# The last store of a fused attention and MLP kernel, issued as two row halves by two queues

## The chip, the cores and the metric

The kernel runs on one core of one Trainium2 chip. The metric is the device time of one execution in microseconds (us), as the median of several runs; lower is better. The profile gives a second number, the span from the first to the last instruction, which is about 1.4 us less than the time (203.0 against 204.4 for the profiled run of the kernel before).

"Tail" below is my word for the stretch from the end of the last VectorE addition to the end of the span. On the path that ends last it holds nothing but the last store and the wait for it, and it can be read from each profile without the scatter of the 200 us ahead of it.

## The reference

```python
x  = A_x                                   # (1, 2048, 640), bfloat16
xn = layernorm(x)
out = x + linear_attention(xn, wqkv, wo)   # 32 heads
        + gelu(xn @ w1 + b1) @ w2 + b2     # hidden width 1536
```

Only the end of this matters here: the output is 2048 token rows of 640 columns, and the last tile of 128 rows is added up and stored in three pieces.

## The kernel before

One planner records instructions for five engines and adds a semaphore wait wherever one engine needs another's result. The stores of the last tile are made in `out_last`: three column pieces of 320, 192 and 128 columns. Each has its matmuls into one bank, one addition by VectorE into `out_l`, and one store that SyncE issues.

```python
def out_last(t):
    xb(t)
    lo = 0
    for i, w in enumerate((HW, 3 * 64, P)):          # 320, 192, 128 columns
        b = take(1)
        hs = slice(lo, lo + w)
        o = out_l[:, hs]
        ...                                          # 17 matmuls into bank b      (L726)
        Pl.ins(v, lambda e, ...: e.tensor_tensor(    # the addition                (L729)
            out=o, in0=bank(b, 0, w), in1=x_res[:, t, hs], op=ALU.add), ...)
        stores.append(Pl.ins("sync", lambda e, hs=hs, o=o:   # the store           (L732)
            e.dma_start(ov[t * P:(t + 1) * P, hs], o), reads=[r_outl[i]], dma=True))
...
for ev in stores[:-1]:
    Pl.wait_event("gpsimd", ev)      # GpSimd waits for all stores but the last
Pl.wait_event("sync", stores[-1])    # SyncE waits for the last                    (L108)
```

The three tiles ahead of the last go through `out_fin`, which makes one addition of 640 columns and one store of 128 rows each, some 5 us apart.

## Time and profile before

| kernel before | |
|---|---|
| time, median of 3 runs | 204.94 us (204.71 to 204.94) |
| span of the profiled run | 203.0 us |
| TensorE busy | 98% of the span |
| last addition ends | 201.54 us |
| tail | 1.51 us |
| last store, from the start of its issue to landing | 1.44 us |

The prediction below shows the lines and how they are read. In a line of the timeline the first number is the start, the second the duration; "SPq" and "ACTq" are the sequencers of SyncE and ScalarE, which issue DMAs. A DMA is "landed" when the last of its steps on its semaphore has come.

### The profile page before, as it was taken

Reading aid. Unit: us, or ns where it says so; the run is one execution under the profiler, and the core shown is the slowest. Engines: PE = TensorE matmul, PEld = TensorE weight load, DVE = VectorE, ACT = ScalarE, POOL = GpSimd, SP = SyncE. Lnnn points to the kernel's source line nnn. Section 1 sums busy time; section 2 is a strip of 40 time slices with the busy share of each in tenths; the row PEclk is TensorE's granted clock in tenths of the full one; section 3 lists DMA queues with packets and bytes.
Section 4 is the critical chain, followed back from the end, with each engine's and each line's share of the span. In section 5 each row is a group of like instructions: output and inputs, shape, how many; then the busy total and the mean of one; then the engine's idle time right before and its main releaser. Section 6 shows DMA issues by size and latency. Waiting matters only on the chain.

```text
span 203.0 us, 3442 instructions
## 1 busy us (share of the span) xinstructions
PE 199.1 (98%) x1317; PEld 121.8 (60%) x1329; DVE 123.0 (61%) x238; ACT 72.8 (36%) x139; POOL 14.4 (7%) x43
## 2 busy tenths in 40 slices
PE   7999999999999999999999999999999999999996
PEld 2799884444457777777756565444444444447775
DVE  4789682000006888999468899896793385356322
ACT  3589886666666544211143596100000000000000
POOL 3145443000000000000000000000000000000000
DMA  5975985999800000000289435115551966084402
GB/s 174 360 259 114 149 181 110 351 275 294 188 0 3 0 0 3 0 0 3 43 273 322 77 66 108 39 29 125 110 116 39 207 106 129 27 196 93 161 32 65
DMA packets 48134, 24.51 MB, mean 121 GB/s; under 512 B 33702, under 2 KB 48118, under 8 KB 48118
## 3 DMA queue, kind: packets, MB, share of 16 engines
q1 hardware_dynamic: 46094, 23.44, 46.4%
q10 hardware_dynamic: 2024, 0.86, 1.7%
q8 instruction: 10, 0.16, 0.3%
q14 instruction: 6, 0.05, 0.1%
HBM read 12.72 MB, written 2.62 MB: 76 GB/s over the span
## 4 chain that ended last, share of the span: by engine, by line
PE 96%; DVE 1%; DMA 1%; issue 0%; DVEq 0%
PE ps L748 27%; PE ps L375 25%; PE ps L524 11%; PE ps L557 11%; PE ps L569 11%; PE ps L690 7%; PE ps L726 2%; PE ps L407 1%; DMA xPK<-in_A_x_dram 1%; DVE stats L331 1%; PE ps L583 1%; PE ps L601 1%; PE ps L396 0%; DVE xn_tm L389 0%; DVE out_l L729 0%
## 5 line engine op out<-in xcount | busy, mean ns | idle before, releaser
L375 PE MATMUL ps<-xnT,W 128*128 128x256 bf16 (+2 forms) x372 | 50.2, 296 | 0.2
L375 PEld LDWEIGHTS ps<-xnT,W 128*128 128x128 bf16 x375 | 32.4, 98 | 17.3
L379 ACT ACTIVATE HG<-ps,b1c 128x256 bf16<-128x256 f32 (+2 forms) x75 | 37.3, 522 | 13.1 <-PE ps L375 11.3
L748 PE MATMUL ps<-HG,W 128*128 128x512 bf16 x177 | 39.2, 379 | 0.2
L748 PEld LDWEIGHTS ps<-HG,W 128*128 128x128 bf16 x180 | 17.6, 98 | 21.2
L569 PE MATMUL ps<-xnT,Wqkv 128*128 128x512 bf16 x96 | 22.2, 379 | 0.2
L524 PE MATMUL ps<-Wqkv,xnT 128*128 128x320 bf16 x160 | 21.9, 299 | 0.0
L557 PE MATMUL ps<-xPK,xn_tm 128*128 128x320 bf16 x160 | 21.9, 299 | 0.0
L524 PEld LDWEIGHTS ps<-Wqkv,xnT 128*128 128x128 bf16 x160 | 15.7, 98 | 6.2
L557 PEld LDWEIGHTS ps<-xPK,xn_tm 128*128 128x128 bf16 x160 | 15.7, 98 | 6.1
L754 DVE SCALAR_TENSOR_TENSOR W<-ps,b2c,xnT 128x512 bf16<-128x512 f32 x15 | 11.3, 751 | 8.9 <-PE ps L748 8.8
L748 PE MATMUL ps<-PQ,Msb 128*128 128x512 bf16 x73 | 16.4, 379 | 0.1
L569 PEld LDWEIGHTS ps<-xnT,Wqkv 128*128 128x128 bf16 x100 | 11.3, 118 | 8.5
L331 DVE BATCH_NORM_STATS2 stats<-xPK 128x6 f32<-128x320 bf16 x32 | 13.7, 468 | 4.4 <-DMA xPK<-in_A_x_dram 4.4
L508 ACT ACTIVATE xn_tm<-ps 128x512 bf16<-128x512 f32 x20 | 11.9, 597 | 9.4 <-PE ps L569 8.7
L511 DVE SCALAR_TENSOR_TENSOR PQ<-ps,xn_tm 128x512 bf16<-128x512 f32 x20 | 13.8, 692 | 2.1
L508 ACT ACTIVATE ek<-ps 128x640 bf16<-128x640 f32 x16 | 11.2, 703 | 9.2 <-PE ps L524 9.2
L511 DVE SCALAR_TENSOR_TENSOR xPK<-ps,ek 128x640 bf16<-128x640 f32 x16 | 13.2, 825 | 1.7
L516 DVE CAST b2c<-out_l 128x5 f32<-128x5 bf16 x1 | 0.2, 172 | 22.4 <-DMA out_l<-b2bc 22.4
L748 PEld LDWEIGHTS ps<-PQ,Msb 128*128 128x128 bf16 x75 | 7.3, 98 | 8.8
L618 DVE SCALAR_TENSOR_TENSOR xn_tm<-PQ,z_sb,xn_tm 128x512 f32<-128x512 bf16 x16 | 12.0, 750 | 0.4
L544 DVE TENSOR_TENSOR Msb<-Msb,xPK 128x640 f32<-128x640 f32 x14 | 11.6, 826 | 0.5
(64 smaller groups left out, 136.1 us busy)
## 6 DMA issues: line engine op xcount, KB each, us to landing
xPK<-in_A_x_dram SPq DMA_DIRECT2D x5, 640.0 KB, 6.9
Wqkv<-in_A_wqkv_dram SPq DMA_DIRECT2D x3, 800.0 KB, 7.0
W<-in_B_w_dram SPq DMA_DIRECT2D x1, 1920.0 KB, 14.8
out_dram<-xPK SPq DMA_DIRECT2D x3, 640.0 KB, 3.6
W<-in_B_w_dram SPq DMA_DIRECT2D x2, 640.0 KB, 6.7
xPK<-in_A_x_dram SPq DMA_DIRECT2D x4, 320.0 KB, 5.9
Wo<-in_A_wo_dram SPq DMA_DIRECT2D x1, 750.0 KB, 11.6
xPK<-in_A_x_dram SPq DMA_DIRECT2D x4, 160.0 KB, 4.4
```

Of the source, the lines that this page charges most:

```text
L331: Pl.ins(v, lambda e: e.bn_stats(stats[:, s, 6 * h:6 * h + 6], x_in[:, t, h * HW:(h + 1) * HW]), reads=[r_x[t]], writes=[r_stats[s][h]])
L375: Pl.ins("tensor", [(lambda e, k=k: e.matmul(bank(b, 0, w), W1[:, k, jb * P:(jb + 1) * P], xnT[:, k, tok], start=(k == 0), stop=(k == DT - ...
L379: Pl.ins("scalar", lambda e: e.activation(HG[:, jb, tok], bank(b, 0, w), ACT.Gelu_apprx_tanh, bias=b1c[:, jb:jb + 1]), reads=[B_[b], r_b1c ...
L508: Pl.ins("scalar", lambda e: e.activation(e2, src, ACT.Exp), reads=br, writes=[re])
L511: Pl.ins(v, lambda e: e.scalar_tensor_tensor(out=d2, in0=src, scalar=0.0, in1=e2, op0=ALU.max, op1=ALU.add), reads=br + [re], writes=[res_ ...
L524: fns.append(lambda e, k=k, h=h, b=b, t=t: e.matmul(bank(b + h, 0, HW), xnT[:, k, t * P:(t + 1) * P], Wqkv[:, k, D + h * HW:D + (h + 1) * ...
L544: Pl.ins(v, lambda e, t=t: e.tensor_tensor(out=zsum, in0=zsum, in1=PK[:, t, :], op=ALU.add), reads=[r_PK[t], r_zsum], writes=[r_zsum])
L557: Pl.ins("tensor", [(lambda e, t=t, h=h, b=b, f=f: e.matmul(bank(b + h, 0, HW), xn_tm[:, t, f * P:(f + 1) * P], PK[:, t, h * HW:(h + 1) * ...
L569: Pl.ins("tensor", [(lambda e, k=k, j=j, b=b: e.matmul(bank(b), Wqkv[:, k, j:D:DT], xnT[:, k, cc], start=(k == 0), stop=(k == DT - 1))) fo ...
L618: Pl.ins(v, lambda e: e.scalar_tensor_tensor(out=yv[c % 2], in0=pq, scalar=z_sb[:, j:j + 1], in1=yv[c % 2], op0=ALU.mult, op1=ALU.add), re ...
L690: return lambda e: e.matmul(bank(b + h, 0, HW), l, r[:, h * HW:(h + 1) * HW], start=(i == 0), stop=(i == JT + DT - 1))
L748: Pl.ins("tensor", lambda e, l=l, r=r, i=i: e.matmul(bank(b), l, r, start=(i == 0), stop=(i == JT + DT - 1)), reads=rd, writes=[B_[b]], ma ...
```

## The change

Its intent is to shorten the tail. The last store, 128 rows of 128 columns, is cut into two halves of 64 rows. ScalarE issues one, SyncE the other, and each queue waits for its own, so that each moves half the bytes.

```diff
-                stores.append(Pl.ins("sync", lambda e, hs=hs, o=o: e.dma_start(ov[t * P:(t + 1) * P, hs], o),
-                                     reads=[r_outl[i]], dma=True))
+                if i < 2:
+                    stores.append(Pl.ins("sync", ...))          # as before
+                    continue
+                for h, eng in ((1, "scalar"), (0, "sync")):
+                    a = h * (P // 2)
+                    stores.append(Pl.ins(eng, lambda e, hs=hs, a=a: e.dma_start(
+                        ov[t * P + a:t * P + a + P // 2, hs], out_l[a:a + P // 2, hs]), reads=[r_outl[i]], dma=True))
...
-        for ev in stores[:-1]:
+        for ev in stores[:-2]:
             Pl.wait_event("gpsimd", ev)
+        Pl.wait_event("scalar", stores[-2])
         Pl.wait_event("sync", stores[-1])
```

More of the change, by code (lines that the diff above doesn't have):

```diff
@@ L731, in out_last @@
                     reads=[B_[b], r_xb[t]], writes=[r_outl[i]])
-                stores.append(Pl.ins("sync", lambda e, hs=hs, o=o: e.dma_start(ov[t * P:(t + 1) * P, hs], o),
-                                     reads=[r_outl[i]], dma=True))
+                if i < 2:
+                    stores.append(Pl.ins("sync", lambda e, hs=hs, o=o: e.dma_start(ov[t * P:(t + 1) * P, hs], o),
+                                         reads=[r_outl[i]], dma=True))
+                    continue
[3 more added lines that the diff above has]
+                        ov[t * P + a:t * P + a + P // 2, hs], out_l[a:a + P // 2, hs]), reads=[r_outl[i]], dma=True))
         def den_parts(c, lo, hi):
```

## The prediction

> **What bounds the kernel now.** I read the views from the coarse to the fine: the busy shares and the chain on the profile page, then the chain of waits in its last microseconds, then the timeline, the wait list of the store queue and the packets of the last store. The page first: columns of its first part are busy microseconds, share of the span, instruction count; the chain is a list of shares.
>
> ```profile
> PE 199.1 (98%) x1317; PEld 121.8 (60%) x1329; DVE 123.0 (61%) x238; ACT 72.8 (36%) x139; POOL 14.4 (7%) x43
> ...
> PE 96%; DVE 1%; DMA 1%; issue 0%; DVEq 0%
> ```
>
> The reader is to see that TensorE sets the time of nearly everything (98% busy, 96% of the chain), and that the change touches none of its instructions: the comparison of instruction orders has the same TensorE, VectorE and GpSimd rows on both sides, line numbers apart. The only additions are one store on ScalarE's queue (64 rows x 128 columns), and the last SyncE store shrinking from 128x128 to 64x128. So only the end can move. The chain of waits for the last 8 us (start, duration, what) and the timeline there (start, duration, engine, line, operation) end as follows.
>
> ```profile
> 196.55 4.67 PE ps L726 x51
> 201.22 0.02 issue
> 201.25 0.29 DVE out_l L729
> ```
>
> ```profile
> 201.25 0.29 DVE L729 TENSOR_TENSOR out_l<-ps,xPK 128x128 bf16<-128x128 f32 x1 [0.59 <-PE ps L726]
> ```
>
> The last addition ends at 201.54; the span is 203.0. Between lies the last store alone: 1.50 us, 0.7% of the span. That is the most that any change to this store could save, and 2% of the time would be 4.1 us. What fills it is in three further views: the wait list of the SyncE queue, the DMA summary of 201.1 to 202.0, and the DMA summary of 202.35 to 202.75 (40 slices of 10 ns each; the digits are tenths of busy DMA engines).
>
> ```profile
> SPq L108 <- DMA out_dram<-out_l: 1.1, 1, 1.1
> ```
>
> ```profile
> out_dram<-out_l SPq DMA_DIRECT2D x1, 32.0 KB, 1.4
> ```
>
> ```profile
> DMA  0000044376588959986694651221100000000000
> ...
> DMA packets 144, 0.03 MB, mean 82 GB/s; under 512 B 144, under 2 KB 144, under 8 KB 144
> ```
>
> SyncE starts the issue at 201.57, spends 0.33 us on it, then waits 1.1 us for the landing. The packets show when: none before 202.39, all done by 202.66, so 0.82 us pass from the start of the issue to the first packet, 0.27 us with packets, and 0.35 us from the last packet to the last of the 16 semaphore steps at 203.01 (1.44 us in all, "1.4" in the line). Only the 0.27 us depends on the size of the store. The 144 packets are 128 rows of 256 B and 16 small ones, one for each of 16 DMA engines; the packet records show a row each 14 ns on one engine, so 8 rows take 0.11 us on an engine, and the engines' last packets are staggered over 0.15 us. The larger stores say the same: 80, 48 and 32 KB land after 1.6, 1.5 and 1.4 us.
>
> **What the Trainium skill says.** The page "DMA: Bandwidth & Descriptors", section "Rules for kernel authors", speaks of exactly this: two transfers to disjoint partition halves "serialize", since both halves spray over all 16 DMA engines. The same page, "Issuing engines are not separate DMA queues", says that starting from several engines saves only the sequencer's issue time. Here one store is split, so there is not even a second issue to save: 0.33 us stays in front of each half. The page's section "Why a DMA increments its semaphore by 16 and not by 1" makes each engine used post its own step, so two halves post 32 rather than 16; the trace has 16 small packets in the 144, which agrees. Its section "Anatomy of one DMA" puts most of a fixed cost of about 2.0 us into the receipt of the written bytes (for another issue path); this trace shows 1.44 in all and only 0.35 after the last packet, so the measured pieces are used.
>
> **The change, part by part.** SyncE's half: the issue stays at 0.33 us (the stores of 1280, 640, 384 and 256 B rows all took 332 to 345 ns when nothing was queued ahead, so bytes don't set it; that rows don't either is my estimate). An engine then has 4 rows instead of 8, which saves 4 x 14 ns = 0.06 us, or up to half the packet stretch, 0.13 us, if the stagger halves too. So this half lands about 1.31 to 1.38 us after issue, earlier than now. This gain counts only if the other half is no later.
>
> ScalarE's half: the trace has pairs issued by both queues at the same moment, with equal size. In the timeline the starts are 176.94 and 176.95, and the DMA summary of 176.9 to 179.6 (queue, bytes, median from issue to landing) has
>
> ```profile
> xn_tm<-rden SPq DMA_DIRECT2D x2, 32.0 KB, 1.9
> xn_tm<-rden ACTq DMA_DIRECT2D x2, 32.0 KB, 2.2
> ```
>
> and the view of that line of the program (min/median/max ns in the issuing queue) has
>
> ```profile
> L643 SPq DMA_DIRECT2D xn_tm<-rden x10: 591/606/1284, 131.6 to 177.6; - x10
> L643 ACTq DMA_DIRECT2D xn_tm<-rden x6: 627/648/856, 141.7 to 177.6; - x6
> ```
>
> ScalarE's issue itself is 0.04 us longer, but its transfer lands 0.3 us later. Where the rest comes from is in two windows that stop early, at 1.50 us after the pair's issue and at 1.35 us after an issue by ScalarE that has no SyncE issue within 0.4 us of it (168.71; this one 64 KB):
>
> ```profile
> q1 hardware_dynamic: 127, 0.03, 9.0%
> q14 instruction: 1, 0.01, 2.1%
> ```
>
> ```profile
> q1 hardware_dynamic: 544, 0.13, 47.3%
> q10 hardware_dynamic: 3, 0.00, 0.4%
> ```
>
> Queue 1 is SyncE's, queue 10 ScalarE's. In the pair, SyncE's queue has moved 127 packets by then and ScalarE's none: its first packet comes 1.54 us after issue, against 1.27 us for SyncE's. Alone, ScalarE's first packets are there after 1.33 us. So ScalarE has a lateness of its own of about 0.06 us, and 0.21 us more when SyncE issues 128 rows in the same moment: something behind the two issues takes them one after the other. I take 0.21 us for 128 rows to be half, 0.10 us, for 64 rows (an estimate; if it is a fixed turn it stays 0.21).
>
> Sum for the half that lands last: 1.44 now, less 0.06 to 0.13 for the halved packets (middle 0.09), plus 0.06 for ScalarE, plus 0.10 for the turn: 1.51 us, so +0.07 us. Its packets also share the engines with SyncE's last ones and 16 more semaphore steps are posted: at the 12 ns that lie between the present steps (16 in 0.18 us), they would cost 0.19 us if both batches came at once; staggered by the turn, most of that is hidden, and I add 0.02. Total +0.09 us. The waits themselves cost nothing new: each queue waits for its own half at the place where SyncE waited anyway, GpSimd still waits for the other 8 stores (its wait for the last of them was over at 202.3), and ScalarE has had no work since 178.5. Nothing earlier moves. Predicted time: 204.94 + 0.09 = about 205.0 us.
>
> **The rivals.** First, the halves really run in parallel: each queue has its own generation and half the packets, so the store ends 0.06 to 0.13 us earlier, and ScalarE's own 0.06 us takes half of that: 204.85 to 204.95. For it speaks that the DMA engines are not full (mean 37.5% in the window above); against it the 0.3 us lateness of every simultaneous pair. Second, the turn is fixed or ScalarE pays what the pairs show in full: 1.44 - 0.09 + 0.30 = 1.65, +0.2 us, 205.15. For it: the pairs' 2.2 against 1.9; against it: those pairs move 128 rows a queue. Third, the end of the program becomes another: the closing exchange between engines may take longer when ScalarE comes last instead of idling there. The trace has no such case; I allow 0.1 us either way. In none of these does an engine become the bound, since TensorE ends at 201.2 in all.
>
> **Range and chances.** The mechanisms span 204.85 to 205.15. The three runs of before lie between 204.71 and 204.94, so a run differs by 0.2 us from the next for nothing, and another session can shift both; I widen to 204.65 to 205.35. Faster by over 2% would need 4.1 us out of a 1.5 us tail: 0.5%. Slower by over 2% would need a transfer of 32 KB to take four times as long: 0.5%. Within 2%: 99%.
>
> **What would show it.** Right, if in the profile of the changed kernel the last addition still ends 0.29 us after its start near 201.25; SyncE's 16 KB lands after 1.3 to 1.4 us, and ScalarE's after 1.45 to 1.6, with its first packets about 0.1 us or more behind SyncE's; and the span is 203.0 to 203.2. The parallel rival is right if both land at 1.4 or below. The fixed turn is right if ScalarE's first packet is 0.27 us behind. I am wrong in kind if ScalarE's issue starts late, if the last addition moves, or if the span and the time part company by more than before (204.4 for the profiled run with a span of 203.0).

## The result and the profile after

The changed kernel took 205.57 us (median of 6 runs, 205.17 to 206.25) against 204.92 us (6 runs, 204.71 to 205.18) for the kernel before. The ratio is 1.0034 with a 95% interval of 1.0014 to 1.0054. By the 2% mark that is "the same", but it is slower clear of the noise, by some 0.65 us, and it lies outside my range, which ended at 205.35.

TensorE is still busy for 98% of the span. The chain of waits of the changed kernel for the last microseconds:

```profile
197.40 4.68 PE ps L726 x51
...
202.10 0.29 DVE out_l L729
```

The 51 matmuls take 4.68 us where they took 4.67, and the addition still takes 0.29 us. So the work of the end is unchanged, but it starts 0.85 us later. Following the offset between the two traces back instruction by instruction, it arises in the first 16 us, in VectorE's wait for loads of x. Here is that group in the wait list of the first 17 us (total us, times, longest), first of the kernel before, then of the changed one:

```profile
DVE stats L331 <- DMA xPK<-in_A_x_dram: 2.4, 2, 1.9
```

```profile
DVE stats L331 <- DMA xPK<-in_A_x_dram: 3.5, 2, 2.0
```

No instruction was changed there. The repeat below shows that most of this part, at least, is chance and not what the change costs. The tail is what it costs. In this profile it is 2.12 us, from 202.39 to 204.51, against 1.51. The timeline and the DMA summary (KB, us from issue to landing) give:

```profile
202.41 0.56 SPq L738 DMA_DIRECT2D out_dram<-out_l  x1
202.42 0.58 ACTq L738 DMA_DIRECT2D out_dram<-out_l  x1
```

```profile
out_dram<-out_l SPq DMA_DIRECT2D x1, 16.0 KB, 1.8
out_dram<-out_l ACTq DMA_DIRECT2D x1, 16.0 KB, 2.1
```

Both issues start within 4 ns of each other, at once after the addition, so neither queue is late to wake. But a half of 16 KB lands later (1.8 us) than the whole of 32 KB did (1.4 us), and ScalarE's half another 0.3 us later. When the packets move is in the DMA summary of 203.59 to 203.99 (slices of 10 ns, digits as in the prediction): SyncE's from 203.63 to 203.86, and ScalarE's, of which the window holds the first 42, from 203.90 on.

```profile
DMA  0000326252756533631431201000000325344665
```

Put together with the packet and semaphore records of both traces, in us:

| piece | before, 128 rows, SyncE | changed, 64 rows, SyncE | changed, 64 rows, ScalarE |
|---|---|---|---|
| issue | 0.333 | 0.558 | 0.582 |
| end of issue to first packet | 0.492 | 0.656 | 0.897 |
| first to last packet | 0.262 | 0.219 | 0.217 |
| last packet to last semaphore step | 0.357 | 0.352 | 0.356 |
| sum, issue to landing | 1.444 | 1.785 | 2.052 |

Below I call the pause between issue and first packet "generation", and the stretch from the last packet to the last semaphore step "receipt". These are names for measured stretches; what happens inside them is not shown.

Halving the rows did shorten the packet stretch, by 0.04 us. The issue became longer by 0.23 us and the pause to the first packet by 0.16 us, for SyncE's half alone; ScalarE's comes a further 0.27 us behind. 0.34 + 0.27 = 0.61 us, which is the growth of the tail and, within noise, of the time (0.65 by the medians, 0.70 by the ratio).

### The profile page after: what moved, and what is told of

Its sections match the earlier page's. It is cut to its first block, busy times and chain, and to the rows that moved or that the text cites. A ratio compares the mean times of both kernels' runs of the same rounds, so it can differ in the third digit from the quotient of the medians.

```text
span 204.5 us, 3456 instructions
## 1 busy us (share of the span) xinstructions
PE 199.8 (98%) x1329; PEld 121.6 (59%) x1329; DVE 122.9 (60%) x238; ACT 73.0 (36%) x139; POOL 14.4 (7%) x43
## 4 chain that ended last, share of the span: by engine, by line
PE 90%; DMA 5%; DVE 2%; SPq 1%; issue 0%; POOL 0%; DVEq 0%
PE ps L754 27%; PE ps L375 21%; PE ps L524 11%; PE ps L557 11%; PE ps L569 11%; PE ps L690 7%; DMA xPK<-in_A_x_dram 3%; PE ps L726 2%; DMA xnT<-xn_tm 1%; DVE stats L331 1%; PE ps L583 1%; PE ps L601 1%; SPq L257 0%; DVE xn_tm L352 0%; SPq L253 0%
## 5 line engine op out<-in xcount | busy, mean ns | idle before, releaser
L569 PE MATMUL ps<-xnT,Wqkv 128*128 128x512 bf16 x100 | 22.8, 379 | 0.0
```

The source lines that it names most:

```text
L569: Pl.ins("tensor", [(lambda e, k=k, j=j, b=b: e.matmul(bank(b), Wqkv[:, k, j:D:DT], xnT[:, k, cc], start=(k == 0), stop=(k == DT - 1))) fo ...
```

## The experiments

Two theories stood at first. **Theory F** (form and turn): a store of 64 rows is issued and generated more slowly than one of 128, whoever issues it (the slow "form"), and of two stores issued at once, ScalarE's has its packets after SyncE's (the "turn"). **Rival Q**: it is the simultaneous issue by two queues that slows both. A third, L, asked whether the change disturbs the loads at the start.

### The changed kernel once more (rep_after)

No edit.

> The changed kernel once more, to tell the reproducible part of the 0.65 us from chance. In the two profiles the tail from the end of the last addition to the end of the span is 2.12 us against 1.50 us before (+0.62), and the last addition itself came 0.85 us later because loads in the first 16 us landed later. Theory F (form and turn: a store of 64 rows is issued and generated more slowly than one of 128, and ScalarE's comes after SyncE's): the tail is again 2.05 to 2.2 us, the issue of each half again 0.55 to 0.60 us, and the time is above the kernel before by about 0.6 us (0.4 to 0.9). Theory L (the loads at the start are disturbed by the change): the last addition is again 0.5 us or more later than in the kernel before. If the start is chance, it lies anywhere within some 0.8 us of it.

Measured: 205.55 us (205.40 to 205.88, 6 runs) against 204.84 us (204.49 to 205.42, 11 runs), ratio 1.0039 (1.0026 to 1.0051). The tail is 2.13 us, and the view of the stores' line (min/median/max ns in the issuing queue) repeats the issue times to 2 ns:

```profile
L738 SPq DMA_DIRECT2D out_dram<-out_l x1: 557/557/557, 202.0 to 202.0; - x1
L738 ACTq DMA_DIRECT2D out_dram<-out_l x1: 580/580/580, 202.0 to 202.0; - x1
```

The last addition ended at 201.95 us, 0.43 us earlier than in the first profile of the same kernel. The kernel before has spans of 203.1 to 204.0 us in these rounds which, less its tail of 1.51 us, puts its last addition at 201.6 to 202.5 us. So theory L falls in the size that it was given: the start scatters in both kernels, and the first profile of the kernel before was at the early end of that scatter. The tail is what repeats. It explains 0.61 us of the 0.7 to 0.8 us of the two ratios; the rest lies within their intervals, so a share of the start of 0.1 to 0.2 us is neither shown nor excluded.

### Both row halves from SyncE (rows_sync)

```diff
-                for h, eng in ((1, "scalar"), (0, "sync")):
+                for h, eng in ((1, "sync"), (0, "sync")):
...
-        Pl.wait_event("scalar", stores[-2])
+        Pl.wait_event("sync", stores[-2])
```

> Both halves of 64 rows from SyncE, one after the other, so no second queue. Theory F: each issue still takes 0.56 us, the first half's packets start 1.2 us after its issue, the second half is issued 0.6 us later and lands 1.79 us after its own issue, so the tail is about 0.03 + 0.60 + 1.79 = 2.4 us, 0.9 us over the kernel before. Rival Q (it is the simultaneous issue by two queues that makes each slow): each issue is 0.33 us again, the second half lands 0.36 us after the first, tail 1.8 us or less, +0.3 us.

Measured: 205.78 us (205.64 to 206.12) against 204.84, ratio 1.0052 (1.0038 to 1.0066), tail 2.49 us.

```profile
L738 SPq DMA_DIRECT2D out_dram<-out_l x2: 562/577/592, 202.0 to 202.6; - x2
DMA to landing us min/median/max: 1.8/1.8/1.8
```

With no second queue at all each half still takes 0.56 and 0.59 us to issue, and the first lands 1.78 us after its issue, as SyncE's half did in the changed kernel (1.785). Rival Q falls. It also follows that ScalarE's company cost SyncE's half nothing.

### Halves by columns instead of rows (cols_two)

```diff
-                    a = h * (P // 2)
-                    stores.append(... ov[t * P + a:t * P + a + P // 2, hs], out_l[a:a + P // 2, hs] ...)
+                    o2 = slice(hs.start + h * (w // 2), hs.start + (h + 1) * (w // 2))
+                    stores.append(... ov[t * P:(t + 1) * P, o2], out_l[:, o2] ...)
```

> The last store in two halves by columns instead of rows, 128 rows x 64 columns each, from the same two queues at the same moment: same bytes a queue, but 128 rows. Theory F: issues are back at 0.33 us (ScalarE some 0.37), SyncE's first packet at 0.83 us, SyncE lands after about 1.4 us, ScalarE's first packet is 0.2 to 0.3 us behind and it lands at 1.6 to 1.75 us; tail 1.65 to 1.8 us, +0.15 to +0.3 us over the kernel before and about 0.4 us under the changed one. Rival Q: issues stay at 0.56 us and more, tail 2.1 us.

Measured: 205.06 us (204.73 to 205.13) against 204.84, ratio 1.0010 (0.9998 to 1.0023), tail 1.69 us, as expected.

```profile
L738 SPq DMA_DIRECT2D out_dram<-out_l x1: 332/332/332, 202.1 to 202.1; - x1
L738 ACTq DMA_DIRECT2D out_dram<-out_l x1: 378/378/378, 202.1 to 202.1; - x1
```

```profile
out_dram<-out_l SPq DMA_DIRECT2D x1, 16.0 KB, 1.4
out_dram<-out_l ACTq DMA_DIRECT2D x1, 16.0 KB, 1.6
```

The same two queues, the same bytes each, 128 rows instead of 64: both issues are fast again, and most of the loss is gone. One part of the expectation fell. ScalarE's first packet comes only 0.07 us behind SyncE's (0.903 us after its issue against 0.829), not 0.2 to 0.3. It still lands 0.2 us later because of the semaphore steps: SyncE's 16 steps run from 1.27 to 1.44 us after the addition and ScalarE's from 1.45 to 1.65 us, one batch directly behind the other, although the last packets of the two stores are only 0.08 us apart.

### The whole last store from ScalarE (act_whole)

```diff
-                stores.append(Pl.ins("sync", lambda e, hs=hs, o=o: e.dma_start(ov[t * P:(t + 1) * P, hs], o),
+                stores.append(Pl.ins("scalar" if i == 2 else "sync", lambda e, hs=hs, o=o: e.dma_start(ov[t * P:(t + 1) * P, hs], o),
...
-        Pl.wait_event("sync", stores[-1])
+        Pl.wait_event("scalar", stores[-1])
```

> The whole last store of 128 rows from ScalarE's queue alone, SyncE's not used for it. It measures ScalarE's own lateness with nothing ahead of it. Theory F: issue 0.35 to 0.38 us, first packet at 0.87 to 0.9 us, landing after 1.5 us, tail 1.55 us, +0.05 us, not to be told from the kernel before in time. If ScalarE's queue is late by 0.27 us for itself (rival S: no turn, the queue is slow), the first packet comes at 1.1 us, landing after 1.7 us, +0.3 us.

Measured: 204.93 us (204.61 to 205.69) against 204.84, ratio 1.0012 (0.9993 to 1.0030), tail 1.57 us.

```profile
L732 ACTq DMA_DIRECT2D out_dram<-out_l x1: 374/374/374, 202.8 to 202.8; - x1
```

The issue is 0.04 us longer than SyncE's, the first packet comes 0.878 us after its start (0.825 for SyncE) and the store lands after 1.50 us. So ScalarE's own lateness is 0.05 us, close to the 0.06 of the prediction, and rival S falls. In the column halves ScalarE's first packet was at 0.903 us, so company cost it only 0.03 us there (its rows were 128 B there and 256 B here; for SyncE the two widths differ by 0.004 us).

### Which row counts are slow (forms_rows, forms_clean, forms_four)

Three kernels use the stores of the tiles ahead of the last, cut into two stores by SyncE with other row counts each. The sum of the rows is always 128, and the output is right. The first, `forms_rows`, issues them directly one behind the other:

```diff
-            stores.append(Pl.ins("sync", lambda e: e.dma_start(ov[t * P:(t + 1) * P, :], out_sb[:, s, :]), ...))
+            a = 0
+            for n in {12: (120, 8), 13: (112, 16), 14: (96, 32)}[t]:
+                stores.append(Pl.ins("sync", lambda e, a=a, n=n: e.dma_start(
+                    ov[t * P + a:t * P + a + n, :], out_sb[a:a + n, s, :]), reads=[r_out[s]], dma=True))
+                a += n
```

> The kernel before, with the stores of the three tiles ahead of the last (5 us apart, off the end of the chain) each cut by rows into two stores by SyncE: 120 and 8 rows, 112 and 16, 96 and 32, all 1280 B wide. Only the first of each pair starts with nothing ahead. It asks which row counts have the slow form (issue 0.56 us, first packet at 1.21 us) and which the fast one (0.33 and 0.83). Theory F1, only 128 rows are fast: all six are slow, 0.55 to 0.60 us. Theory F2, eight rows on each engine used are fast: the Trainium skill has a store use the largest number of engines up to 16 that divides its rows, so 120 rows are 15 engines of eight rows and fast, while 112 (seven each) and 96 (six each) are slow. Theory F3, the cost falls or rises with the number of rows: 112 and 96 lie between 0.33 and 0.56. The last store is as before, tail 1.5 us.

112 rows took 0.322 us to issue and 96 rows 0.316 us. F1 and F2 both fall, and so does F3, which had them between 0.33 and 0.56: these are as fast as 128 rows. The other four stores were issued close behind another one and are not clean. So the next two kernels wait for the first store of a pair to land before the second is issued:

```diff
+                if a:
+                    Pl.wait_event("sync", stores[-1])
...
+            for n in {12: (112, 16), 13: (80, 48), 14: (32, 96)}[t]:      # forms_clean
+            for n in {12: (120, 8), 13: (72, 56), 14: (40, 88)}[t]:       # forms_four
```

> The run before this one gave 0.32 us of issue for 112 rows and 0.32 for 96, both as fast as 128, so neither F1 (only 128 rows are fast) nor F2 (only eight rows an engine) holds, and 64 rows (0.52 to 0.56 us in every run) stand out. Here six row counts on SyncE, each store started only after the one before it has landed, so that each is clean: 112 and 16, 80 and 48, 32 and 96 rows. Theory F4, four rows or fewer on each of 16 engines are slow (64, and so 48, 32 and 16): 80 and 96 take about 0.31 us with the first packet at 0.8, while 48, 32 and 16 take 0.5 us or more with the first packet at 1.2. Theory F5, 64 rows alone have the slow form: all six take 0.28 to 0.33 us, first packet 0.78 to 0.83 us.

> The same with row counts that 16 does not divide: 120 and 8, 72 and 56, 40 and 88. By the Trainium skill's rule they use 15, 8, 12, 14, 10 and 11 engines, that is 8, 1, 6, 4, 4 and 8 rows on each. Theory F4 (rows on each engine decide): 56, 40 and 8 are slow (0.5 us and more), 120, 72 and 88 are fast (0.3 us). If the total of rows decides with a limit between 64 and 80: 72 may go either way, 56, 40 and 8 slow, 88 and 120 fast. Theory F5 (64 alone): all fast.

The rule on the number of engines, in these expectations, stands in the Trainium skill, page "DMA: Bandwidth & Descriptors", section "Why a DMA increments its semaphore by 16 and not by 1". This case's trace agrees: the stores of 8, 56, 40 and 88 rows in forms_four show one jump of the semaphore at about 0.46 us after issue and then 8, 14, 10 and 11 steps.

From the timelines (start, duration), first of forms_clean, for its store of 32 rows, then of forms_four, for those of 56 and 40 rows:

```profile
198.17 0.31 SPq L716 DMA_DIRECT2D out_dram<-out_sb  x1
```

```profile
195.16 0.32 SPq L716 DMA_DIRECT2D out_dram<-out_sb  x1
...
197.68 0.28 SPq L716 DMA_DIRECT2D out_dram<-out_sb  x1
```

| rows | 8 | 16 | 32 | 40 | 48 | 56 | 64 | 88 | 96 | 112 | 128 |
|---|---|---|---|---|---|---|---|---|---|---|---|
| issue, us | 0.29 | 0.33 | 0.31 | 0.28 | 0.31 | 0.32 | **0.56** | 0.29 | 0.32 | 0.32 | 0.33 |
| first packet, us after start of issue | 0.78 | 0.85 | 0.82 | 0.76 | 0.81 | 0.80 | **1.21** | 0.78 | 0.81 | not read | 0.83 |

(64 and 128 rows are from the changed kernel and the kernel before. 72, 80 and 120 rows came directly behind another store and are left out; 80 follows on the path below. For 112 rows packets of earlier stores were still running.) Theory F4, four rows or fewer to an engine, falls with 56, 48, 40, 32, 16 and 8 rows. What stands is F5: of all row counts tried, 64 alone is slow. Counts close to 64 (57 to 71) were not tried.

### 64 rows at other places and widths (forms_64)

```diff
+            for n, (a, z, lo, hi) in enumerate({12: ((0, 128, 0, D),), 13: ((32, 96, 0, D), (0, 32, 0, D), (96, 128, 0, D)),
+                                                14: ((0, 64, 0, 64), (0, 64, 64, D), (64, 128, 0, D))}[t]):
+                if n:
+                    Pl.wait_event("sync", stores[-1])
+                ...                                   # SyncE stores rows a to z, columns lo to hi
```

> Whether the slow form belongs to 64 rows wherever they lie. Off the end of the chain, each store started after the landing of the one before: tile 13 in rows 32 to 95, then 0 to 31, then 96 to 127; tile 14 in rows 0 to 63 of 64 columns, rows 0 to 63 of the other 576 columns, then rows 64 to 127. If the count of 64 is what counts, all four stores of 64 rows take 0.52 to 0.57 us to issue with the first packet at 1.2 us, and the two of 32 rows 0.31 us and 0.81 us. If it is the halves' place (a half of the partitions, 0 to 63 or 64 to 127), rows 32 to 95 take 0.31 us.

The timeline shows rows 32 to 95 at 193.45, then 32 rows at 195.47, and the 64 rows of 64 columns at 198.07:

```profile
193.45 0.64 SPq L716 DMA_DIRECT2D out_dram<-out_sb  x1
...
195.47 0.36 SPq L716 DMA_DIRECT2D out_dram<-out_sb  x1
...
198.07 0.54 SPq L716 DMA_DIRECT2D out_dram<-out_sb  x1
```

The other two stores of 64 rows took 0.49 and 0.47 us, and all four had their first packet 1.12 to 1.29 us after the start of issue. The two of 32 rows took 0.36 and 0.33 us. So among these stores the count of 64 is what matters, not the place or the width; the issue time itself ranges more widely (0.47 to 0.64) than I expected.

### ScalarE's extra 0.27 us (forms_pairs)

```diff
+            parts = {12: (("scalar", 64, 128, 0, D), ("sync", 0, 64, 0, D)),
+                     13: (("scalar", 0, 128, HW, D), ("sync", 0, 128, 0, HW)),
+                     14: (("scalar", 64, 128, 0, D), ("sync", 0, 64, 0, D))}[t]
+            for n, (eng, a, z, lo, hi) in enumerate(parts):
+                if t == 14 and n == 1:
+                    Pl.wait_event("sync", stores[-1])
+                ...                                   # engine eng stores rows a to z, columns lo to hi
```

> The kernel before, with three stores ahead of the last changed off the end of the chain: tile 12 in row halves by both queues at once (the slow form, with a turn expected), tile 13 in column halves by both at once (the fast form), tile 14 in row halves, ScalarE's first and SyncE's only after ScalarE's has landed. The question is whether ScalarE's extra 0.27 us belongs to its queue or to the company of SyncE's store. Theory turn: in tile 12 ScalarE's first packet comes 1.48 us after issue, in tile 14, alone, after 1.21 + 0.05 = 1.26 us. Theory slow queue: 1.48 us in both. Tile 13: issues of 0.33 and 0.38 us, first packets at 0.83 and 0.9 us as in the column halves of the last store.

Tile 12 did not do what it was built for: SyncE was still busy with earlier work, so ScalarE's half was issued alone, 1.4 us ahead of SyncE's. It serves as a second case of ScalarE alone. In tile 14 SyncE's half was issued at 199.88, after ScalarE's had landed. ScalarE's, from the timeline:

```profile
197.78 0.54 ACTq L718 DMA_DIRECT2D out_dram<-out_sb  x1
```

Alone, ScalarE's 64 rows had their first packet 1.195 us (tile 14) and 1.220 us (tile 12) after the start of issue; in the company of SyncE's 64 rows it was 1.479 and 1.480 us (changed kernel and its repeat). So some 0.27 us belong to the company, as the turn theory says, and not to the queue. The stores alone had rows of 1280 B and those in company 256 B; by forms_64 first packets of 64 rows differ by up to 0.17 us among themselves, so the 0.27 is good to no better than that. In the fast form the turn is shorter: 0.03 us in the last store's column halves. In tile 13 (rows of 640 B) ScalarE's first packet came 0.16 us behind SyncE's (1.013 against 0.849), of which 0.05 is ScalarE's own lateness.

### Row parts that avoid 64 (rows_80_48, rows_88_40)

```diff
-                for h, eng in ((1, "scalar"), (0, "sync")):
-                    a = h * (P // 2)
+                for eng, a, z in (("scalar", 80, P), ("sync", 0, 80)):     # 88 in rows_88_40
                     stores.append(Pl.ins(eng, lambda e, hs=hs, a=a, z=z: e.dma_start(
                         ov[t * P + a:t * P + z, hs], out_l[a:z, hs]), reads=[r_outl[i]], dma=True))
```

> The changed kernel with one number changed: the last store is cut into 80 rows for SyncE and 48 for ScalarE instead of 64 and 64. Theory F5 (64 rows alone have the slow form; 80 and 48 rows were issued in 0.31 to 0.33 us off the path): issues 0.31 and 0.36 us, first packets at 0.81 and about 0.88 us, 32 semaphore steps one behind the other at 12 ns, so ScalarE's last lands 1.6 us after issue, tail 1.65 us, time +0.1 to +0.25 us over the kernel before and about 0.45 us under the changed kernel. Theory 'two queues by rows' (cutting by rows for two queues is what costs): tail 2.1 us as in the changed kernel, +0.65 us.

Measured: 205.42 us (204.90 to 206.57) against 204.93 (204.53 to 205.63, 11 runs), ratio 1.0019 (1.0004 to 1.0035). The runs scatter over 1.7 us, so the time alone does not decide. The profiled run was its slowest, with a last addition that ended at 203.47, but its tail does decide: 1.71 us, 0.42 us shorter than in the changed kernel.

```profile
L737 SPq DMA_DIRECT2D out_dram<-out_l x1: 345/345/345, 203.5 to 203.5; - x1
L737 ACTq DMA_DIRECT2D out_dram<-out_l x1: 377/377/377, 203.5 to 203.5; - x1
```

```profile
out_dram<-out_l SPq DMA_DIRECT2D x1, 20.0 KB, 1.4
out_dram<-out_l ACTq DMA_DIRECT2D x1, 12.0 KB, 1.6
```

Still two queues, still a cut by rows; only the number 64 is gone, and the slow form and the long turn are gone with it (first packets at 0.841 and 0.912 us).

> The same with 88 rows for SyncE and 40 for ScalarE: by the Trainium skill's rule these use 11 and 10 engines, so only 21 semaphore steps are awaited instead of 32. It asks whether the steps are what is left of the loss. First packets at 0.78 and 0.85 us; if the steps follow one another at 12 ns from about 1.24 us, the last comes at 1.24 + 0.25 = 1.49 us, tail 1.53 us, the same as the kernel before. If the steps are not what counts, it lands as the 80/48 split does, tail 1.65 us.

Measured: 204.75 us (204.61 to 205.91) against 204.93, ratio 1.0001 (0.9982 to 1.0021): not to be told from the kernel before. The tail of its profile is 1.71 us, though, not the 1.53 that I expected. The 21 awaited steps run from 1.36 to 1.67 us after the addition, ScalarE's first and SyncE's mostly behind them. Fewer steps did not end earlier, so how much of the remaining loss the number of steps makes is left open.

No version tried beats the kernel before. Its tail is 1.51 us; that of ScalarE alone is 1.57, of the column halves 1.69, of 80/48 and 88/40 rows 1.71, of the changed kernel 2.12 and 2.13, and of two halves on SyncE 2.49.

## Why the prediction was wrong

**The frame held.** The tail alone is concerned, TensorE bounds the rest and neither queue starts late. One sign of being wrong in kind, "if the last addition moves", did appear (0.85 us in the first profile), but the repeat puts it down to scatter of the start. The direction (slightly slower) and the class (within 2%, given 99%) were right. The size was not: +0.09 us foretold, +0.65 us measured, outside the range.

**The step that failed first** is the one on SyncE's half: "bytes don't set it; that rows don't either is my estimate". Bytes indeed don't: all fast stores with nothing directly ahead took 0.28 to 0.38 us. For rows the estimate fails at exactly the number that the change uses. The issue measured 0.558 us instead of 0.33, and the first packet came 1.21 us after issue instead of 0.83. Where the prediction let SyncE's half land after 1.31 to 1.38 us, it landed after 1.785. This term is 0.34 us over the kernel before and about 0.44 us over the middle of the prediction. Nothing in the profile before shows a store of 64 rows, so the profile could not have told; it could have told me to widen the range for a form that it does not contain.

**The second is the turn**: "I take 0.21 us for 128 rows to be half, 0.10 us, for 64 rows (an estimate; if it is a fixed turn it stays 0.21)". The mechanism was right, shown by ScalarE alone (1.20 to 1.22 us to the first packet) against ScalarE in company (1.48). The size was not halved: it measured 0.27 us (which holds whatever lateness of its own ScalarE has in this form; 0.06 and 0.10 were foretold for the two together). The pairs that I took it from had issues of 0.6 us and first packets at 1.27 us themselves. They are not stores of 128 rows to HBM, the chip's main memory: by the kernel's code each copies 32 rows within SBUF, the on-chip memory, and reads each row four times. Looked at now, they resemble the slow form, while with fast stores of 128 rows of 128 B the turn is only 0.03 us. That the pairs and the 64 rows are slow for the same reason is an inference that no run here tests.

**The gain term** was of the right kind but small: 0.06 to 0.13 us foretold, 0.04 us measured.

**ScalarE's own lateness** was right in its number: 0.06 us foretold, 0.05 us measured with a fast store. Luck had a part in it: the 1.33 us "alone" is of a copy from another line, with twice the bytes, and its first packet came at 170.04, just after packets of SyncE's transposes had ended at 170.01, so ScalarE's queue was not alone there.

**The semaphore steps**: I added 0.02 us, expecting the turn to hide them. In the changed kernel that holds: ScalarE's steps begin at 1.91 us after the addition, SyncE's are over at 1.81. Once the turn is gone, as in the column halves, they show: ScalarE's last step comes 0.49 us after its last packet instead of 0.36.

**The rivals.** The parallel one (204.85 to 204.95) did not happen. The fixed turn: 0.27 us is what I wrote as its sign, and it was there, but that is luck too. The turn is not fixed (0.03 us in fast stores), and its total of 205.15 us lacked the slow form. The third, a longer closing exchange, did not happen: the time less the span is 1.4 us in both kernels.

**The Trainium skill.** Its advice in "DMA: Bandwidth & Descriptors", section "Rules for kernel authors", not to bother with disjoint partition halves is borne out by the result and by the unequal parts of rows_80_48 and rows_88_40, none of which is faster than one store; the halves by columns of cols_two are not either. But the reason that it gives, the sharing of the 16 engines, is not what cost the time here: the packets of the halves took 0.22 us each, without overlap, and those of the whole 0.26. The cost was ahead of the packets.

**What stays open** is why 64 rows are slow, and why the turn is long with that form and short with the other. The runs show where the time goes (issue, generation, turn), not what makes them long.

## What to carry to other kernels

When a store at the very end of a kernel is as small as this one, most of its time does not shrink with it: issue, generation and receipt made 1.18 of 1.44 us here and the packets 0.26, of which the cut won 0.04. The cut pays for that with a second queue's lateness, its turn and its semaphore steps. Before a DMA is cut into a shape that the trace does not contain yet, measure that shape somewhere off the path in the same kernel: the issue time of one such store would have warned of it. And for a change of the last microsecond compare tails, not whole times, since the loads at the start scatter by more than the effect.

## What the Trainium skill lacked or had wrong

- No page that I found says that a store of 64 rows from SBUF to HBM is issued more slowly than one with fewer or more rows. Measured: 0.47 to 0.64 us against 0.28 to 0.38 us for 8, 16, 32, 40, 48, 56, 80, 88, 96, 112 and 128 rows with nothing directly ahead, and a first packet at 1.12 to 1.29 us against 0.76 to 0.88 (ScalarE's of a simultaneous pair left out). It belongs to "DMA: Bandwidth & Descriptors".
- The same page, section "Latency and other measured facts", gives about 0.6 us to the first byte for SyncE's and ScalarE's path. Counted from the start of the issue instruction, the fast form here took 0.83 us and the slow one 1.21; counted from its end, 0.49 and 0.66. The page does not say from where it counts.
- The same page, section "Issuing engines are not separate DMA queues", says that the transfers interleave. Elsewhere the page says that the two queues have no descriptor generator of their own, but it gives no time for the turn that simultaneous issues take ahead of the first packet (0.03 us for two fast stores of the last tile, 0.27 us for two of 64 rows), nor does it say that the semaphore steps of two stores that finish together come one batch behind the other, as in cols_two (16 steps from 1.27 to 1.44 us, the next 16 from 1.45 to 1.65).
- A fetch of instructions seems to hold up one DMA engine at the wrong moment. No page that I read gives a cost for it. In forms_rows, forms_clean and forms_four the unchanged last store landed after 2.0 us instead of 1.44. Its steps came on time but for the last, which was 0.5 to 0.6 us late. In forms_rows the last eight rows started 1.18 us after issue, just as an 8 KB packet of queue 14, of the kind "instruction", that had begun at 0.88 us was over; in the other two runs eight rows likewise start within 5 ns of such a packet's end. That both were on one DMA engine is inferred from this. It explains the late rows, but only part of the late step: from the last packet to the last step 0.71 to 0.74 us passed instead of 0.36, and why is open.
